# A recurrent attention with a feed-forward behind it: chunk 0 in two units of two batches, second masks on GpSimd or VectorE, and another table of order

## Chip, core, metric

One core of one Trainium2 chip runs the whole program. The metric is the device time of one execution in microseconds (us). Eight executions of the kernel before gave 171.22 to 172.64 us, median 172.0.

## What is computed

Four batches, 8 heads, 768 steps, head size 48. Each head keeps a 48x48 state; at every step it is read with r, decayed by w and increased by the outer product of k and v; the present step enters the output with the weight u. The 3072 x 384 result goes through a feed-forward without a nonlinearity:

```python
for t in range(S):
    kt, vt, rt, wt = (k[:, :, t], v[:, :, t], r[:, :, t], w[:, :, t])
    cur = np.einsum('bhd,bhe->bhde', u[None] * kt, vt)
    y[:, :, t] = np.einsum('bhd,bhde->bhe', rt, state + cur)
    state = wt[:, :, :, None] * state + np.einsum('bhd,bhe->bhde', kt, vt)
...
x = y.transpose(0, 2, 1, 3).reshape(B * S, H * D)      # 3072 x 384
out = ((x @ w1) * (x @ w2)) @ w3 @ w_out               # 384 -> 1024 -> 1024 -> 384
```

## The kernel before

**Tiling.** The 768 steps are cut in six chunks of 128. A *unit* is one chunk of one or two batches, and `UNITS` lists them as (chunk, first batch, batches): chunk 0 has units 0 and 1 of one batch each and unit 2 of two, the other chunks two units of two batches, 13 units in all. A *block* of the feed-forward takes the tokens of one unit (chunk 0) or of two (`BLOCKS`): 128, 128, 256 and five times 512 tokens. w3 and w_out are multiplied once, in the kernel, to w34 (`w34_block`, eight pieces: transpose of a w3 piece L627, product with w_out L639, each copied out by ScalarE or VectorE), so that a block is two products (x w1 and x w2, L938), their product elementwise (ScalarE copies one out, L947; VectorE multiplies it with the other, L951) and one matmul with w34 (L960), copied out (L968) and stored (L973).

**A unit** (`unit`). ScalarE takes the logarithm of w (ln, L669). TensorE forms cumulative sums with the triangle LT, once by rows (cs, L678) and once transposed (ct, L685). ScalarE takes their exponentials (ne, L692; e, L698). VectorE scales k (Kt, L703). TensorE transposes r (trr, L767) and the scaled k (trk, L786); VectorE multiplies r's transpose by e (RT, L772), and ScalarE or VectorE copies k's (KT, L791). TensorE forms the scores of each batch (m, L805). They are masked to the strict lower triangle (msk): VectorE multiplies them from PSUM by a mask (L811), or ScalarE copies them to SBUF (L814) and GpSimd masks them there in place (maff, L817). The tile is Mbf. TensorE multiplies scores by v (y, L849) and, from chunk 1 on, r by the state (ys, L840).

The diagonal term goes another way. r times k (rk, L708) is weighted by u: in the units of chunk 0 (`PE_DIAG`) TensorE transposes rk (L721), multiplies by a block matrix of u (d, L735), and the sums are copied (dcp, L740); elsewhere rk is multiplied by a broadcast u (ruk, L743) and reduced (dg, L747). The result scales v (dv, L749), and VectorE adds the output of y to it (yb, L861). yb is transposed (yt, L878), copied to xT (L883) and feeds the block. State: k times v (kv, L895), added (T, L902), decayed (S, L906), converted (Sc, L908). In the last four units the three transposes are DMAs on SyncE's queue.

u is one row. It is loaded by GpSimd's queue (L543); TensorE spreads it to all partitions (ub, L548 and L550), VectorE and GpSimd build the block matrix from it (ublk, L559 to L565).

**Loads.** `load` brings rows of w, k, r, v of a unit (in chunk 0) or of four batches (later), L579; `wload` brings halves of w1 and w2, quarters of w3, and w_out, L586. All go on GpSimd's queue, but for those in `SP_LOADS`, w of units 0 and 1, on SyncE's. A GpSimd load occupies GpSimd while it is issued. `LOADS` gives them their turn.

**Order.** Nothing is issued where it stands in the text. Each step is put in a list by `op` with its engine, a nominal duration, what it reads and writes, and a number, the sum of three: `prio` from the text, `RANK` of its kind, `STEP` of its name. `schedule` then walks along a nominal time; on each engine, of the steps that are ready and have room in PSUM (`CAPS`), it takes the one of the lowest number. `ENGINE` says on which engine a step runs that has a choice. Each engine executes its list strictly in that order. The tables `RANK`, `STEP` and `ENGINE` are long and are not shown in full; a load's number is

```python
return -10000.0 + (LOADS.index(key) if key in LOADS else 1000 + 10 * int(key.split("_")[1]) + "wkrv".index(key[0]))
```

plus its `STEP`. The triangle LT and the identity I are finished by GpSimd among its loads (L502, L506), the mask by VectorE (L511).

Of the kernel before, what the change touches and what calls it, by code (L numbers as in the profile page):

```python
# [27 lines left out]
    "table": 91258, "ones": 70780, "I128": 2.5, "pads": 147127.5, "rpads": 129663.5, "state0": 193483,  # L28
    "mask": 114325.5, "u": 6, "ub": 85613, "ubc": 115778.5, "ublk": 139994.5, "ublk2": 139582.5, "w1_0": -1,
    "w2_0": -9, "w2_1": 1, "w3_0": -2, "w3_1": -1, "gate": 18300.5, "wt_0": 186936.5, "w3Te_0": 180388.5,  # L30
    "wm_0": 14284.5, "w34e_0": 196262, "wt_1": 188036.5, "w3Te_1": 184064.5, "wm_1": 14355, "w34e_1": 199640,
    "wt_2": 187264.5, "w3Te_2": 180421.5, "wm_2": 16664.5, "w34e_2": 193580, "wt_3": 190065, "w3Te_3": 183294.5,
    "wm_3": 16602.5, "w34e_3": 193341, "wt_4": 190831, "w3Te_4": 186363.5, "wm_4": 21086.5, "w34e_4": 199881.5,
    "wt_5": 190040.5, "w3Te_5": 178239.5, "wm_5": 17262, "w34e_5": 199838.5, "wt_6": 190773, "w3Te_6": 178710.5,
    "wm_6": 22072.5, "w34e_6": 191892.5, "wt_7": 196434, "w3Te_7": 186247.5, "wm_7": 26850, "w34e_7": 198902,
    "rpad3": 110949.5, "win_0": 9, "kin_0": 2, "rin_0": 1, "vin_0": 7, "ln_0": 30931, "cs_0": 150610.5,
    "ct_0": 76350, "ne_0": 143756.5, "e_0": 168276.5, "Kt_0": 277987.5, "rk_0": 5791.5, "rkt_0": 141899.5,
    "rke_0": 160559, "d_0": 138446.5, "dcp_0": 35270, "dv_0": 113183, "trr_0": 168163.5, "RT_0": 130924.5,
    "trk_0": 151420, "KT_0": 176728.5, "m_0_0": 123125, "msk_0_0": 159784, "maff_0_0": 263427.5, "y_0": 179238.5,
    "yb_0": 262883.5, "yt_0": 197545, "xT_0": 274692.5, "kv_0": 92018.5, "T_0": 197296, "S_0": 111557.5,  # L40
    "Sc_0": 119238.5, "a_0_0": 101744, "b_0_0": 93277, "asb_0_0": 161353.5, "abT_0_0": 286641, "a_0_1": 101961,
    "b_0_1": 93964, "asb_0_1": 159579.5, "abT_0_1": 291543.5, "o_0_0": 5590.5, "osb_0_0": 193613.5,
    "store_0_0": 6002.5, "win_1": -4, "kin_1": -5, "rin_1": 3, "vin_1": 5, "ln_1": 30947, "cs_1": 150772,
    "ct_1": 76143, "ne_1": 141159, "e_1": 168318, "Kt_1": 277556.5, "rk_1": 4519, "rkt_1": 141823.5, "rke_1": 161966,
    "d_1": 138542.5, "dcp_1": 37096, "dv_1": 113323.5, "trr_1": 168113, "RT_1": 133329, "trk_1": 151647,
    "KT_1": 179246.5, "m_1_0": 122337.5, "msk_1_0": 159570.5, "maff_1_0": 264349, "y_1": 178903.5, "yb_1": 268439,
    "yt_1": 198092, "xT_1": 270303.5, "kv_1": 92554.5, "T_1": 197456.5, "S_1": 111049, "Sc_1": 120091,
    "a_1_0": 101694.5, "b_1_0": 94039.5, "asb_1_0": 159924.5, "abT_1_0": 286673, "a_1_1": 101907.5, "b_1_1": 94046.5,
    "asb_1_1": 159555.5, "abT_1_1": 287058, "o_1_0": 5697.5, "osb_1_0": 183614.5, "store_1_0": 6383, "win_2": -2,
    "kin_2": -10, "rin_2": -9, "vin_2": 4, "ln_2": 27502, "cs_2": 150899, "ct_2": 77090, "ne_2": 140677,  # L50
    "e_2": 165156, "Kt_2": 277775, "rk_2": 8720.5, "rkt_2": 141179, "rke_2": 159467, "d_2": 138283.5, "dcp_2": 42304,
    "dv_2": 112314.5, "trr_2": 168851, "RT_2": 128671.5, "trk_2": 151531.5, "KT_2": 175478, "m_2_0": 122874.5,
    "msk_2_0": 157605, "maff_2_0": 263855, "m_2_1": 122898.5, "msk_2_1": 162959.5, "maff_2_1": 263536,
    "y_2": 179372.5, "yb_2": 263117, "yt_2": 197797.5, "xT_2": 277998.5, "kv_2": 92588.5, "T_2": 193231,
    "S_2": 110815, "Sc_2": 121324.5, "a_2_0": 102140, "b_2_0": 94251, "asb_2_0": 159794, "abT_2_0": 289379,
    "a_2_1": 103972, "b_2_1": 93111, "asb_2_1": 159681.5, "abT_2_1": 289610, "a_2_2": 101093.5, "b_2_2": 94164.5,
    "asb_2_2": 161243.5, "abT_2_2": 291851.5, "a_2_3": 101827.5, "b_2_3": 93487.5, "asb_2_3": 158664.5,
    "abT_2_3": 291948, "o_2_0": -5503.5, "osb_2_0": 183340.5, "store_2_0": 5875, "o_2_1": 5884.5, "osb_2_1": 182980,
    "store_2_1": 6211.5, "win_3": -3, "vin_3": 3, "ln_3": 27848, "cs_3": 151181, "ct_3": 77556, "ne_3": 140780.5,
    "e_3": 165597.5, "Kt_3": 275543.5, "rk_3": 7878.5, "ruk_3": 74734.5, "dg_3": 9567.5, "dv_3": 75124,  # L60
    "trr_3": 167958, "RT_3": 129021.5, "trk_3": 151855, "KT_3": 178411.5, "m_3_0": 125437, "msk_3_0": 155155,
    "maff_3_0": 225704.5, "m_3_1": 123078.5, "msk_3_1": 160746, "maff_3_1": 264622, "ys_3": 21875, "y_3": 179345,
    "yb_3": 268271.5, "yt_3": 197961.5, "xT_3": 270309, "kv_3": 96277, "T_3": 198817, "S_3": 115528,
    "Sc_3": 123788.5, "ln_4": 27267, "cs_4": 150936.5, "ct_4": 77248, "ne_4": 140824, "e_4": 165405.5,
    "Kt_4": 281230, "rk_4": 7858, "ruk_4": 75130, "dg_4": 6720.5, "dv_4": 116166.5, "trr_4": 168619, "RT_4": 128759,
    "trk_4": 150933.5, "KT_4": 176652.5, "m_4_0": 122915.5, "msk_4_0": 157299, "maff_4_0": 264522.5, "m_4_1": 122692,
    "msk_4_1": 164510, "maff_4_1": 225906, "ys_4": 19313, "y_4": 178859, "yb_4": 268194, "yt_4": 201240.5,
    "xT_4": 274660.5, "kv_4": 96164.5, "T_4": 190408, "S_4": 116763, "Sc_4": 127066, "a_3_0": 110805.5,
    "b_3_0": 107195.5, "asb_3_0": 166326, "abT_3_0": 284054, "a_3_1": 105385.5, "b_3_1": 97538, "asb_3_1": 166241.5,
    "abT_3_1": 284607, "a_3_2": 114695, "b_3_2": 106576.5, "asb_3_2": 166344, "abT_3_2": 297320.5, "a_3_3": 109704,  # L70
    "b_3_3": 107425.5, "asb_3_3": 165812.5, "abT_3_3": 284217.5, "o_3_0": 3065, "osb_3_0": 189965,
    "store_3_0": -13643.5, "o_3_1": -3540.5, "osb_3_1": 182912, "store_3_1": 6189, "o_3_2": 3720.5,
    "osb_3_2": 178613.5, "store_3_2": -13244.5, "o_3_3": 3864.5, "osb_3_3": 190066.5, "store_3_3": -13873,
    "win_5": 92762.5, "kin_5": 92899.5, "rin_5": 93432, "vin_5": 127145.5, "ln_5": 27637.5, "cs_5": 154048.5,
    "ct_5": 83867, "ne_5": 148436.5, "e_5": 172207, "Kt_5": 281438, "rk_5": 3786.5, "ruk_5": 77301, "dg_5": 9607.5,
    "dv_5": 74252, "trr_5": 175681.5, "RT_5": 143863, "trk_5": 159034, "KT_5": 176385.5, "m_5_0": 124511,
    "msk_5_0": 172521, "maff_5_0": 225963, "m_5_1": 131175, "msk_5_1": 162305.5, "maff_5_1": 260791, "ys_5": 20907,
    "y_5": 191985.5, "yb_5": 260626.5, "yt_5": 210295.5, "xT_5": 276599, "kv_5": 94241, "T_5": 191553,
    "S_5": 109235.5, "Sc_5": 126032.5, "ln_6": 34632, "cs_6": 154367, "ct_6": 84620.5, "ne_6": 147704.5,
    "e_6": 170579, "Kt_6": 281133.5, "rk_6": 19597.5, "ruk_6": 77271.5, "dg_6": 1840.5, "dv_6": 74062.5,  # L80
    "trr_6": 181449.5, "RT_6": 126707, "trk_6": 159283.5, "KT_6": 183212.5, "m_6_0": 135160.5, "msk_6_0": 161986,
# [969 lines left out]
```

## Time and profile before

| | |
|---|---|
| median of 8 executions | 172.0 us (171.22 to 172.64) |
| the profiled execution | 172.34 us, span 170.6 us |
| TensorE (PE) busy | 155.2 us, 91%, 1732 matmuls |
| VectorE (DVE) busy | 120.9 us, 71% |
| GpSimd (POOL) busy, issue of loads included | 106.8 us, 63% |
| ScalarE (ACT) busy | 98.0 us, 57% |
| granted TensorE clock | 1.00 throughout |
| moved by DMA | 24.12 MB, 141 GB/s on average |
| chain that ended last | PE 85%, POOL 4%, DMA 4%, DVE 3%, issue 2%, ACT 1% |

How to read it: the span is the time from the first to the last instruction of one profiled execution; the execution's own time is a little longer. Busy time is the sum over an engine's instructions. A line of a group names the source line, the engine, the operation, output and inputs with their shapes, how often it occurred, then busy time and mean duration, and after the second bar the idle time of the engine just before it and what ended it. In the chain each piece is followed back to what released it. "DMA to landing" is from the start of the issuing instruction to the completion of the transfer.

### The profile page before, as it was taken

The page shows a single profiled execution, that of the slowest core. Times are in us where ns is not written, and L with a number is a line of the kernel's source. Part 1 is how long each engine was busy: PE and PEld are TensorE (multiplying, and loading weights), DVE is VectorE, ACT ScalarE, POOL GpSimd, SP SyncE. Part 2 cuts the span into 40 slices and gives each one's busy share as a digit, 9 for nine tenths or more (in the row PEclk, how much of TensorE's full clock was granted, in tenths as well). Part 3 has the DMA queues.
Part 4 walks back from the last instruction along what each step waited for, and adds up shares of the span by engine and source line. Part 5 has one row for each costly group of instructions (what it writes and reads, how often), then busy time and mean ns, then how long its engine had stood idle before and what let it go on. Part 6 is the DMA issues. An engine that isn't in the chain of part 4 may idle for free.

```text
span 170.6 us, 4149 instructions
## 1 busy us (share of the span) xinstructions
PE 155.2 (91%) x1732; PEld 99.9 (59%) x1732; DVE 120.9 (71%) x156; ACT 98.0 (57%) x134; POOL 106.8 (63%) x90
## 2 busy tenths in 40 slices
PE   0543899999999999999999999999999999999991
PEld 0332679998677576656655576456556554455550
DVE  6254899886886689798899987898796770633330
ACT  4522458788754778536869888645574425233311
POOL 7999497975996898999967999915533200000000
PEclk9999999999999999999999999999999999999999
DMA  5999999999999999999999992957365222011132
GB/s 98 134 196 188 225 174 146 167 187 181 180 229 150 144 144 122 131 227 205 169 197 259 152 180 72 136 134 164 82 122 147 96 60 80 4 46 46 46 126 107
DMA packets 96364, 24.12 MB, mean 141 GB/s; under 512 B 88633, under 2 KB 94265, under 8 KB 96345
## 3 DMA queue, kind: packets, MB, share of 16 engines
q0 software_dynamic: 79024, 15.86, 117.7%
q1 hardware_dynamic: 17320, 8.00, 18.7%
q8 instruction: 13, 0.21, 0.5%
q14 instruction: 7, 0.05, 0.1%
HBM read 27.79 MB, written 4.72 MB: 191 GB/s over the span
## 4 chain that ended last, share of the span: by engine, by line
PE 85%; POOL 4%; DMA 4%; DVE 3%; issue 2%; ACT 1%; POOLq 0%; DVEq 0%
PE banks L938 36%; PE banks L960 19%; PE banks L639 6%; PE banks L805 4%; DMA u_row<-in_u_dram 4%; PE banks L849 3%; PE banks L685 3%; PE banks L627 2%; PE banks L895 2%; PE banks L678 2%; PE banks L878 2%; POOL kin L579 2%; PE banks L767 2%; PE banks L786 2%; PE banks L840 1%
## 5 line engine op out<-in xcount | busy, mean ns | idle before, releaser
L938 PE MATMUL banks<-xT,w_bf 128*128 128x512 bf16 (+2 forms) x384 | 68.3, 327 | 0.1
L938 PEld LDWEIGHTS <-w_bf 128*128 128x128 bf16 x384 | 32.8, 98 | 25.4 <-issue 0.6
L951 DVE TENSOR_TENSOR abT<-a_sb,banks 128x1024 bf16<-128x1024 f32 (+1 forms) x28 | 29.7, 1067 | 22.1 <-PE banks L938 18.4
L947 ACT COPY a_sb<-banks 128x1024 f32<-128x1024 f32 (+1 forms) x28 | 24.8, 891 | 16.6 <-PE banks L938 15.6
L960 PE MATMUL banks<-w,abT 128*128 128x384 bf16 x192 | 33.9, 327 | 0.0
L960 PEld LDWEIGHTS <-abT 128*128 128x128 bf16 x192 | 18.3, 98 | 12.8
L968 ACT COPY osb<-banks 128x384 f32<-128x384 f32 x19 | 9.1, 478 | 20.0 <-PE banks L960 18.5
L817 POOL TENSOR_SCALAR_AFFINE_SELECT Mbf<-Mbf 128x1024 bf16<-128x1024 bf16 x12 | 13.0, 1093 | 9.5 <-ACT Mbf L814 9.4
L749 POOL TENSOR_TENSOR dv<-vin,dg 128x768 bf16<-128x768 bf16 (+1 forms) x9 | 12.9, 1443 | 9.0 <-DMA xT<-dv 5.1
L811 DVE TENSOR_TENSOR Mbf<-banks,mask 128x1024 bf16<-128x1024 f32 x12 | 14.6, 1220 | 4.1 <-PE banks L805 2.9
L814 ACT CAST Mbf<-banks 128x1024 bf16<-128x1024 f32 x12 | 12.1, 1017 | 5.4 <-PE banks L805 5.4
L698 ACT ACTIVATE eT<-banks 128x1024 f32<-128x1024 f32 (+1 forms) x13 | 12.5, 959 | 3.1 <-PE banks L685 3.1
L703 DVE TENSOR_TENSOR Kt<-kin,banks 128x768 bf16<-128x768 bf16 (+1 forms) x11 | 9.6, 878 | 5.5 <-DMA kin<-in_k_dram 4.6
L685 PE MATMUL banks<-LT,lw 128*128 128x128 bf16 x96 | 8.3, 234 | 5.5 <-POOL LT L502 5.1
L708 POOL TENSOR_TENSOR rk<-rin,kin 128x768 bf16<-128x768 bf16 x8 | 13.1, 1638 | 0.2 <-DMA rin<-in_r_dram 0.2
L861 DVE TENSOR_TENSOR dv<-banks,dv 128x768 bf16<-128x768 f32 (+1 forms) x13 | 11.6, 893 | 1.7 <-PE banks L849 1.3
L692 ACT ACTIVATE banks<-banks 128x768 f32<-128x768 f32 (+1 forms) x13 | 9.7, 750 | 4.5 <-PE banks L678 4.5
L579 POOL DMA_DIRECT2D vin<-in_v_dram x7 | 10.0, 1423 | 2.6 <-issue 2.6
L772 DVE TENSOR_TENSOR KRT<-banks,eT 128x1024 bf16<-128x1024 bf16 (+1 forms) x9 | 9.9, 1103 | 2.1 <-PE banks L767 1.1
L639 PE MATMUL banks<-wo_bf,w3T 128*128 128x384 bf16 x64 | 11.4, 327 | 0.0
L579 POOL DMA_DIRECT2D kin<-in_k_dram x7 | 10.0, 1436 | 1.1 <-POOLq L1035 0.8
L685 PEld LDWEIGHTS <-lw 128*128 128x128 bf16 x96 | 6.8, 105 | 6.4 <-ACT lw L669 4.3
(92 smaller groups left out, 234.3 us busy)
## 6 DMA issues: line engine op xcount, KB each, us to landing
out_dram<-osb SPq DMA_DIRECT2D x24, 192.0 KB, 2.0
win<-in_w_dram POOLq DMA_DIRECT2D x4, 768.0 KB, 8.8
w_bf<-in_moe_w_dram POOLq DMA_DIRECT2D x4, 512.0 KB, 7.5
w_bf<-in_moe_w_dram POOLq DMA_DIRECT2D x4, 384.0 KB, 7.7
kin<-in_k_dram POOLq DMA_DIRECT2D x4, 384.0 KB, 7.9
rin<-in_r_dram POOLq DMA_DIRECT2D x4, 384.0 KB, 8.1
vin<-in_v_dram POOLq DMA_DIRECT2D x4, 384.0 KB, 8.4
wo_bf<-in_moe_w_out_dram POOLq DMA_DIRECT2D x1, 768.0 KB, 8.6
```

Source lines behind the costliest of these rows:

```text
L579: op(eng, 60 if eng == "SP" else 650 + 270 * nb, lambda: e.dma_start(dst[:, b0 * H:(b0 + nb) * H, :D], ap), late=SP_ROWS if src == "w" and ...
L639: nc.tensor.matmul(o[:, :DM], lhsT=w3T[fi % 2][:, gi, :], rhs=wo_bf[:, gi, :], start=(gi == 0), stop=(gi == FI - 1))
L685: nc.tensor.matmul(o[:, b, q, :], lhsT=LW[:, b * H + 2 * q:b * H + 2 * q + 2, :].rearrange("t h d -> t (h d)"), rhs=LT, start=True, stop=True)
L698: nc.scalar.activation(ET[:, :, 1:], o[:, :nb * HP, :], Act.Exp)
L708: op("DVE", {"DVE": dve(N, 2), "POOL": 1490}, lambda e: ENG[e].tensor_mul(rks, rr[:, :, :D], kk), r=[*kr, *kk_], w=[f"rk{s}"], prio=pr + 8 ...
L749: op("POOL", {"POOL": 100 + 1.8 * N, "DVE": dve(N)}, lambda e: ENG[e].tensor_mul(dvs, vv, dgs[:, :, None].to_broadcast([C, bh, D])), r=[f" ...
L811: nc.vector.tensor_mul(Mbf[m].rearrange("s j q t -> s (j q t)"), o.rearrange("s j f -> s (j f)"), mask.rearrange("s q t -> s (q t)"))
L817: nc.gpsimd.affine_select(Mbf[m].rearrange("s j q t -> s (j q) t"), Mbf[m].rearrange("s j q t -> s (j q) t"), compare_op=Alu.is_gt, fill=0 ...
L938: nc.tensor.matmul(o[:, q * T // TB, q % (TB // T), :], lhsT=wt[:, di, fi * P:(fi + 1) * P], rhs=xT[x][:, di, :T], start=(di == 0), stop=( ...
L947: nc.scalar.copy(a_sb[sa][:, :nbk * TB], banks[:, g.at(A):g.at(A) + nbk, :].rearrange("p k t -> p (k t)"))
L951: nc.vector.tensor_mul(abT[x][:, f[0]:f[0] + G, :T].rearrange("p i t -> p (i t)"), a_sb[sa][:, :nbk * TB], banks[:, g.at(Bk):g.at(Bk) + nb ...
L960: nc.tensor.matmul(banks[:, g.at(O), :DM], lhsT=abT[x][:, fi, tt * P:(tt + 1) * P], rhs=w34[:, fi, :], start=(fi == 0), stop=(fi == FI - 1))
```

## The change

- Chunk 0 has two units of two batches. There are 12 units (numbered 0 to 11), and the blocks of chunk 0 have 256 tokens each. Unit 1 now holds what unit 2 held. The sets that name units are shifted with it.
- SyncE loads w of unit 0 (two batches in one DMA); all else is on GpSimd's queue.
- The halves of w1 and w2 come before the rows of chunk 1 in `LOADS`. (The sizes of the weight pieces stay: `WP` is 2, `W3P` is 4.)
- The second step of a mask that ScalarE copied out can run on VectorE, as a product with the mask in SBUF.
- `RANK`, `STEP` and `ENGINE` are replaced, so the order of all engines changes. By the new `ENGINE`, 9 masks are made by VectorE from PSUM and 15 copied by ScalarE; of those, 10 are masked by GpSimd and 5 by VectorE.

```diff
 STEP = {
...
+    "w3Te_0": 179236, "wm_0": 28425, "w34e_0": 182625, "wt_1": 203756.5, "w3Te_1": 171253, "wm_1": 28573.5,
...
 ENGINE = {
...
+    "rke_0": "DVE", "dcp_0": "ACT", "dv_0": "DVE", "KT_0": "ACT", "msk_0_0": "DVE", "maff_0_0": "POOL",
+    "msk_0_1": "ACT", "maff_0_1": "DVE", "xT_0": "DVE", "S_0": "DVE", "osb_0_0": "DVE", "osb_0_1": "ACT",
...
-LOADS = """win_0 kin_0 u rin_0 vin_0 win_1 kin_1 rin_1 vin_1 win_2 kin_2 rin_2 vin_2
-w1_0 w2_0 w1_1 w2_1 win_3 kin_3 rin_3 vin_3 wo w3_0 w3_1 w3_2 w3_3""".split()
-
-UNITS = [(0, 0, 1), (0, 1, 1), (0, 2, 2)] + [(c, b, 2) for c in range(1, 6) for b in (0, 2)]
-
-DMA_KR = set(range(9, 13))
-DMA_Y = set(range(9, 13))
-DMA_R = set(range(9, 13))
-PE_DIAG = {0, 1, 2}
+LOADS = """win_0 kin_0 u rin_0 vin_0 win_1 kin_1 rin_1 vin_1 w1_0 w2_0 w1_1 w2_1
+win_2 kin_2 rin_2 vin_2 wo w3_0 w3_1 w3_2 w3_3""".split()
+
+UNITS = [(0, 0, 2), (0, 2, 2)] + [(c, b, 2) for c in range(1, 6) for b in (0, 2)]
+
+DMA_KR = set(range(8, 12))
+DMA_Y = set(range(8, 12))
+DMA_R = set(range(8, 12))
+PE_DIAG = {0, 1}
...
-BLOCKS = [[0], [1], [2], [3, 4], [5, 6], [7, 8], [9, 10], [11, 12]]
-
-SP_LOADS = {("w", 0), ("w", 1)}
+WP, W3P = 2, 4
+
+BLOCKS = [[0], [1]] + [[t, t + 1] for t in range(2, 12, 2)]
+
+SP_LOADS = {("w", 0)}
...
-            def maff(m=m):
+            def maff(e, m=m):
+                if e == "DVE":
+                    nc.vector.tensor_mul(Mbf[m].rearrange("s j q t -> s (j q) t"), Mbf[m].rearrange("s j q t -> s (j q) t"), mask)
+                    return
                 nc.gpsimd.affine_select(Mbf[m].rearrange("s j q t -> s (j q) t"), Mbf[m].rearrange("s j q t -> s (j q) t"),
                                         compare_op=Alu.is_gt, fill=0.0, base=0, channel_multiplier=-1,
                                         pattern=[[0, 2 * HP], [1, C]])
...
-            op("POOL", 1110 * by_act, maff if by_act else lambda: None, r=[f"M{m}"], w=[f"M{m}"], prio=pr + 7 + b,
+            op("POOL", {"POOL": 1110 * by_act, "DVE": 690 * by_act}, maff if by_act else lambda e: None, r=[f"M{m}", "mask"], w=[f"M{m}"], prio=pr + 7 + b,
                name=f"maff_{t}_{b}", port=True)
```

The loads up to chunk 1, in the order of their numbers (those in brackets are on SyncE's queue; LT and I stand among them by their own numbers):

| | |
|---|---|
| before | kin_2, kin_1, (win_1), rin_2, LT, kin_0, rin_0, w2_0, I, win_2, u, (win_0), rin_1, vin_0, w1_0, vin_1, win_3, w1_1, vin_2, w2_1, kin_3, rin_3, w3_0, wo, w3_1, vin_3, w3_2, w3_3 |
| after | kin_0, rin_0, vin_0, LT, win_1, I, kin_1, (win_0), u, rin_1, vin_1, w1_0, w2_0, w2_1, w1_1, win_2, w3_0, kin_2, rin_2, wo, w3_1, w3_2, w3_3, vin_2 |

In a name such as kin_2 the number is the unit's; from chunk 1 on the load of a chunk's first unit brings all four batches (win_3 before is win_2 after).

## The prediction

> **What bounds the kernel now.** I read the slices of the page first, then busy time by stretch, then TensorE's own waits, then the chain that ended last. In the slices (one digit is the busy share of 4.27 us, in tenths) TensorE is the row to watch:
>
> ```profile
> PE   0543899999999999999999999999999999999991
> DVE  6254899886886689798899987898796770633330
> POOL 7999497975996898999967999915533200000000
> ```
>
> From the sixth slice to the last but one TensorE is full; before that it is not. The stretches give the size (columns: stretch, its length, then PE, PEld, DVE, ACT, POOL busy, granted clock, DMA share, GB/s):
>
> ```profile
> 5.00:10.00 5.00, 2.29 (x15) 1.43 (x15) 1.83 (x4) 2.45 (x5) 5.00 (x8) 1.00 2.43 139
> 10.00:15.00 5.00, 1.94 (x19) 1.60 (x20) 2.50 (x4) 0.58 (x1) 5.00 (x6) 1.00 1.52 203
> 15.00:20.00 5.00, 4.19 (x48) 2.92 (x48) 3.47 (x9) 2.18 (x5) 2.75 (x6) 1.00 1.34 223
> 20.00:25.00 5.00, 4.62 (x55) 3.89 (x52) 4.97 (x6) 2.53 (x4) 5.00 (x4) 1.00 1.62 188
> 30.00:40.00 10.00, 10.00 (x153) 9.22 (x151) 8.17 (x11) 8.17 (x11) 7.06 (x6) 1.00 1.35 182
> 160.00:170.60 10.60, 7.20 (x44) 4.01 (x41) 2.89 (x4) 1.41 (x3) 0.00 (x0) 1.00 0.26 95
> ```
>
> TensorE is idle 15.44 us of 170.6 (170.6 - 155.16): 5.00 before the first matmul, 2.71 + 3.06 + 0.81 + 0.38 up to 25 us, 0.1 up to 160, and 3.4 at the end, where the last copy and store follow the last matmul. Nothing is to be had in the middle; the start is the only stretch with idle TensorE, and DMA and GpSimd's issues fill it. TensorE's waits name the causes:
>
> ```profile
> PE banks L685 <- POOL LT L502: 5.1, 1, 5.1
> PE banks L548 <- DMA u_row<-in_u_dram: 2.7, 1, 2.7
> PE banks L786 <- DVE Kt L703: 2.6, 2, 1.4
> ```
>
> The chain shows how the start ends (start, length, what):
>
> ```profile
> 8.92 6.19 DMA u_row<-in_u_dram
> ...
> 18.29 1.23 DVE Mbf L811
> ...
> 20.74 2.06 DVE dv L749
> ...
> 25.18 1.58 PE banks L938 x24
> ...
> 27.82 0.67 PE banks L938 x12
> ...
> 36.92 0.65 PE banks L938 x6
> ```
>
> The row u lands at 15.1; from there the diagonal term, dv, yb, yt and xT lead to the first feed-forward matmul at 25.18.
>
> **TensorE's total: nothing.** Units (0,0,1) and (0,1,1) become one, with the same matmuls per batch. Only the feed-forward of chunk 0 changes form: 96 matmuls of 128 columns and 48 of 256 become 96 of 256. The chain has 12 of 128 in 0.67 (56 ns) and 6 of 256 in 0.65 (108 ns), so 96 x 0.056 = 5.4 us become 48 x 0.108 = 5.2: 0.2 gained. The Trainium skill (TensorE: Matmul & The Clock Gate, Back-to-back issue gap) gives about 81 ns for a 128-column matmul with its weight load; by it the narrow form would cost 7.8 us and the change would gain 2.6. The row is from this very line, so I take 0.2.
>
> **Masks.** The rows that price them:
>
> ```profile
> L811 DVE TENSOR_TENSOR Mbf<-banks,mask 128x1024 bf16<-128x1024 f32 x12 | 14.6, 1220 | 4.1 <-PE banks L805 2.9 <-issue 1.1
> L814 ACT CAST Mbf<-banks 128x1024 bf16<-128x1024 f32 x12 | 12.1, 1017 | 5.4 <-PE banks L805 5.4
> L817 POOL TENSOR_SCALAR_AFFINE_SELECT Mbf<-Mbf 128x1024 bf16<-128x1024 bf16 x12 | 13.0, 1093 | 9.5 <-ACT Mbf L814 9.4
> L511 DVE TENSOR_TENSOR mask<-LT,I 128x1024 bf16<-128x1024 bf16 x1 | 0.7, 693 | 0.0
> ```
>
> By the engine table, direct masks on VectorE go from 12 to 9, ScalarE copies from 12 to 15; behind these, GpSimd masks 10 and VectorE 5. The new form has no row; L511, same shape and types, gives 0.69. (Bounds: not below this; 1.22 if it ran at L811's pace, 2.7 us for five, on an engine with 50 us idle.) VectorE: -3 x 1.22 + 5 x 0.69 = -0.2; GpSimd -2 x 1.09 = -2.2; ScalarE +3 x 1.02. With all other reassignments in the table, priced from the same rows, VectorE has +1.6 us, ScalarE -3.1, GpSimd -1.7. What matters is the crowded stretch, 60 to 100 us, where VectorE is busy 36.3 of 40 us and GpSimd 36.8. For the four units of chunks 2 and 3: VectorE +2.8 (four second masks) +0.5 (rk) -1.3 (ruk) -1.9 (S) -0.6 (xT) = -0.5; GpSimd -4.4 (masks) -1.6 +3.3 +1.9 = -0.8. So TensorE's cover holds and this costs nothing. A VectorE mask waits for ScalarE's copy, and the abT and yb behind it wait too; a miss costs at most the 1.02 of one copy each, five in all.
>
> **The load queue.** A load's place is -10000 plus its index in LOADS plus STEP. Before, GpSimd issues the rows of unit 2 first (kin_2, kin_1, rin_2), then LT, kin_0, rin_0, w2_0, I, win_2, u. After: kin_0, rin_0, vin_0, LT, win_1, I, kin_1, u, rin_1, vin_1, then w1_0, w2_0, w2_1, w1_1, win_2, w3_0, kin_2, rin_2, wo, w3_1 to w3_3, vin_2. (Unit 1 after holds the batches of unit 2 before.) SyncE's two loads of w become one of two batches, which I put at 4.4, where the second of the two lands now. On GpSimd k, r and v of batches 0 and 1 are one issue of 1.2 us each instead of two of 0.9: 1.8 less. Asked one at a time, the loads of before land: kin_2 6.5, rin_2 8.5, kin_0 9.3, rin_0 10.0, u 15.1, w1_0 17.7, win_3 21.8, w2_1 26.7, kin_3 29.8, rin_3 32.1, wo 39.1, vin_3 45.4, w3_3 50.8; successive landings stand 1.3 us apart for two batches of rows and some 2 us for a w1 or w2 half. In the new order this gives estimates of kin_0 6.5, rin_0 7.8, vin_0 9.1, LT 5.35 (5.06 now), win_1 10.9, kin_1 12.3, u 14.0 (ends 12.6 and 14.4: GpSimd issues it at 8.2, and u now takes 6.2), vin_1 15.1, w1_0 17.2, w2_0 19.2, w1_1 23.3 to 24.8, win_2 26.4, kin_2 32, rin_2 34.5, wo 38.7, w3_3 47, vin_2 50. So chunk 0's rows come earlier, w3 too, and chunk 1's rows later: w and v by 4.6 us, k and r by 2.3.
>
> **The start, after.** ln needs both batches: 4.45 to 5.3, so cs begins at 5.4 (5.11 now) but for two batches; Kt ends near 9.2 for both (9.9 now), RT and KT near 10.4, scores at 11.4. u then decides. From u's landing to the first feed-forward matmul it takes 10.0 us now, of which the steps themselves are 4.9 and 5.1 is queueing: Mbf 1.23 and Kt 0.95 ahead on VectorE, and dv at 2.06 where the row of 768 elements elsewhere shows 0.96. After, steps for two batches are 5.5 (u 0.74, ublk 0.7, d 0.35, dg 0.2, dv 0.96, yb 0.96, yt 0.5, xT 0.55, nine handovers of 0.06). Of the queueing I keep half, 2.5, as two units compete and not three. First feed-forward matmul: 14.0 + 5.5 + 2.5 = 22.0.
>
> What counts is time minus work done. Warm pieces of the chain give 8.4 us for all of chunk 0's attention and u. Chain and idle from 25.18 to 167.21 leave 5.7 done by 25.18: 19.5 lost. After, at 22.0, of unit 1 the scores, y, kv, d and yt are open (1.9): 6.5 done, 15.5 lost. Gain 4.0.
>
> **What is given back.** TensorE at the start runs at half pace:
>
> ```profile
> 20.85 1.03 PE L767 MATMUL banks<-I,rin 128*128 128x128 bf16 x8
> ...
> 35.86 0.61 PE L767 MATMUL banks<-I,rin 128*128 128x128 bf16 x8
> ```
>
> The same eight transposes take 1.03 and then 0.61; now it is warm from 25.5. The Trainium skill (same page, What's actually happening) speaks against this change: full pace comes after about 3.4 us of sustained work, and an idle window of that length takes it away. By it the 3.4 us after 22.0 run at half pace: 1.7 lost. By the rows alone (dense from 19.6, warm at 25.5) it can be up to 2.9, or nothing if unit 1's attention has warmed it. I take 0.8. Between 30 and 50 us TensorE lives on rows of chunk 1 and the w3 work as they land; I take 0.4 for gaps (0 to 2.5). Sum: 4.0 + 0.2 - 0.8 - 0.4 = 3.0. The profiled execution was 172.34 (span 170.6 and 1.74 around it), so 169.3 for such a one; the median of eight is 172.0, so **169.0**.
>
> **Rivals.** *Loads late* (0.20): w1_1 and win_2 come behind four weight halves; feed-forward 0 stops after its first half, TensorE waits to 24.8, cools, and again for kin_2 and wo. For it: every load issued from 12.86 to 17.02 us took 8.9 to 9.7 to land. Against: before has a similar queue and no wait on it after 16 us. Price 1.5 + 0.8 more: 171.3. *u decides as now* (0.08): u lands at 15 and the queueing stays 5.1; feed-forward at 25.6 with 6.5 to 7 done, 172 within 0.5: no change. *Slower* (0.17): vin_2 is last on GpSimd's queue, behind masks and dv. From v's landing to chunk 1's first feed-forward now passes 9.3 us (45.4 to 54.74). TensorE's other work (8.4 + 10.4 feed-forward 0 + 14.0 w3 work + 7.4 attention 1 + 5.2 outputs 0 = 45.4, with 15.5 lost) lasts until 60.9, so vin_2 later than 51.6 costs its lateness, and later than about 54.6 all the gain; GpSimd has waited 5.5 us at once for a mask's copy. At 57: 174.4. Against: a backlog of some 6 us of transfers covers such a wait. *Main case* (0.55): 167.4 to 170.6.
>
> **Chances and range.** A measurement tells 0.3% from no change, some 0.5 us. Faster: 0.53 of the main case, 0.18 of late loads, 0.02 of the third, together 0.73; same 0.02 + 0.01 + 0.04 = 0.07; slower 0.17 + 0.01 + 0.02 = 0.20. From 166.8 (no loss to cold or gaps, u at 12.6) to 173.4, which leaves most of the slow case and a little below out.
>
> **What would show it.** Right: the first L938 near 22; u landing near 14; TensorE's idle sum near 12.5; no L938 wait for w_bf; L811 x9, L814 x15, L817 x10 and five bf16 masks near 0.7. Wrong: TensorE idle between 25 and 60 us, waits of vin or abT, five masks well over 1 us, or a first L938 after 24.

## The result, and the profile after

The changed kernel takes **171.28 us** (median of 18 runs, 170.55 to 171.82); the kernel before 171.99 us (53 runs, 171.22 to 173.15). The ratio is 0.995, 95% interval 0.9934 to 0.9966: faster by 0.7 us, where the prediction had 3.0 us. The ratio of a variant, below, is taken against runs of the kernel before made together with it; ratios leave out executions over 1.5% slower than the fastest of their kernel, which medians count. Its profiled execution took 171.36 us with a span of 169.6; that of before 172.34 with 170.6.

Lines have moved in kernel.py: the feed-forward products L938 are now L942, the w34 product L960 is L964, the cumulative sums L685 and L678 are L686 and L679, the transposes L767 and L786 are L768 and L787, the scores L805 are L806, the masks L811, L814, L817 are L812, L815, L821, and L819 is VectorE's second mask. The other lines move by 1 ahead of the masks and by 4 behind them: y is L853, yb L865, yt L882, kv L899.

The slices of the page, each now 4.24 us:

```profile
PE   0488899998999999999799999999998999999991
DVE  5378786788367999997898999985896573415510
POOL 7995589069989987997999999526332400000000
```

TensorE is fuller in slices 3 to 5 than it was (4 3 8 before, 8 8 8 now), but there are now slices below 9 behind the sixth: the tenth, the twentieth, the thirty-first. Those were all 9 before. Busy time by stretch (stretch, length, then PE, PEld, DVE, ACT, POOL busy, granted clock, DMA share, GB/s):

```profile
10.00:15.00 5.00, 3.74 (x56) 2.70 (x54) 3.79 (x7) 3.47 (x5) 3.12 (x5) 1.00 2.36 150
20.00:25.00 5.00, 4.28 (x49) 3.33 (x48) 4.45 (x6) 2.95 (x5) 4.43 (x4) 1.00 1.14 240
25.00:30.00 5.00, 4.81 (x61) 3.92 (x60) 2.74 (x5) 3.92 (x6) 4.38 (x5) 1.00 1.83 180
30.00:40.00 10.00, 9.32 (x140) 7.99 (x140) 8.44 (x11) 8.41 (x12) 4.72 (x4) 1.00 1.73 189
80.00:100.00 20.00, 18.89 (x202) 11.09 (x199) 17.25 (x21) 16.08 (x21) 19.39 (x14) 1.00 2.02 180
160.00:169.60 9.60, 6.05 (x38) 3.43 (x35) 1.99 (x3) 1.44 (x3) 0.00 (x0) 1.00 0.28 103
```

TensorE is idle 14.5 us (169.6 less 155.1), 0.9 less than before; 12.5 was forecast. Up to 25 us idle time fell from 12.0 to 8.4. But from 25 to 160 us it grew from 0.1 to 2.5: 0.19 in 25 to 30, 0.68 in 30 to 40, 1.11 in 80 to 100, 0.53 in 120 to 140.

TensorE's own waits:

```profile
PE banks L679 <- POOL LT L503: 5.4, 1, 5.4
PE banks L549 <- DMA u_row<-in_u_dram: 1.3, 1, 1.3
PE banks L882 <- DVE dv L865: 1.1, 1, 1.1
PE banks L768 <- DMA rin<-in_r_dram: 1.1, 1, 1.1
PE banks L942 <- DVE xT L887: 0.7, 1, 0.7
```

The wait for u has gone from 2.7 to 1.3, and Kt's 2.6 is off the list. New are L882 (yt), 1.1 us for yb (L865, written into the tile dv), which itself waits for GpSimd's dv (L750), and 0.5 us of the scores L806 for a ScalarE mask copy (L815):

```profile
PE banks L806 <- ACT Mbf L815: 0.5, 1, 0.5
```

The chain that ended last now runs through the middle of the kernel on other engines than TensorE:

```profile
7.85 5.54 DMA u_row<-in_u_dram
...
22.08 10.05 DMA kin<-in_k_dram
...
74.49 1.49 POOL dv L750
...
77.21 1.72 POOL kin L580
...
79.81 1.44 POOL dv L750
```

**Where the gain was, and where it went.** Idle time does not see a TensorE that runs at half pace. So I also took the elapsed time less the work done: each matmul of the trace counts with its own form's start-to-start time at full pace (56 ns for 128 columns, 109 for 256, 162 for 384, 216 for 512), and the rest is lost. (A few records are missing in traces, which makes it uncertain by some 0.2 us.)

| us lost by | 25 us | 40 | 60 | 80 | 90 | 120 | 160 |
|---|---|---|---|---|---|---|---|
| before | 19.0 | 19.75 | 20.6 | 21.3 | 21.1 | 22.7 | 23.5 |
| after | 14.8 | 16.8 | 17.5 | 18.35 | 19.6 | 21.35 | 22.6 |
| gain | 4.2 | 2.95 | 3.1 | 2.95 | 1.5 | 1.35 | 0.9 |

The start brings 4.2 us. 1.3 goes back between 25 and 40 us, nothing from 40 to 80, 1.4 between 80 and 90, 0.6 later (0.53 of it idle at 128 us, behind one multiplication on VectorE that took 2.44 us instead of 1.21 beside a GpSimd operation; in the traces of five variants it took 1.22, so this part is one execution's).

### The profile page after: what moved, and what is told of

It reads as the page before. It is cut to its first block, busy times and chain, and to the rows that moved or that the text cites. A ratio compares the mean times of both kernels' runs of the same rounds, so it can differ in the third digit from the quotient of the medians.

```text
span 169.6 us, 4034 instructions
## 1 busy us (share of the span) xinstructions
PE 155.1 (91%) x1684; PEld 99.0 (58%) x1684; DVE 120.9 (71%) x156; ACT 96.2 (57%) x124; POOL 102.6 (60%) x85
## 4 chain that ended last, share of the span: by engine, by line
PE 68%; POOL 12%; DMA 11%; issue 4%; DVE 2%; ACT 1%; POOLq 0%; DVEq 0%
PE banks L942 26%; PE banks L964 16%; PE banks L640 6%; DMA kin<-in_k_dram 6%; DMA u_row<-in_u_dram 3%; POOL dv L750 3%; PE banks L853 2%; POOL kin L580 2%; PE banks L686 2%; PE banks L806 2%; PE banks L787 2%; PE banks L679 2%; PE banks L768 2%; DMA KRT<-Kt 2%; PE banks L628 2%
## 5 line engine op out<-in xcount | busy, mean ns | idle before, releaser
L942 PE MATMUL banks<-xT,w_bf 128*128 128x512 bf16 (+1 forms) x336 | 67.8, 349 | 1.2 <-DVE xT L887 0.7
L942 PEld LDWEIGHTS <-w_bf 128*128 128x128 bf16 x336 | 31.7, 98 | 27.1 <-issue 1.6
L951 ACT COPY a_sb<-banks 128x1024 f32<-128x1024 f32 (+1 forms) x28 | 24.9, 890 | 26.2 <-PE banks L942 23.5
L964 PE MATMUL banks<-w,abT 128*128 128x384 bf16 x192 | 34.5, 326 | 0.0
L964 PEld LDWEIGHTS <-abT 128*128 128x128 bf16 x192 | 18.1, 98 | 12.6
L821 POOL TENSOR_SCALAR_AFFINE_SELECT Mbf<-Mbf 128x1024 bf16<-128x1024 bf16 x10 | 11.0, 1097 | 12.6 <-ACT Mbf L815 11.7
L750 POOL TENSOR_TENSOR dv<-vin,dg 128x768 bf16<-128x768 bf16 x9 | 13.2, 1476 | 7.6 <-DMA xT<-dv 5.5
L815 ACT CAST Mbf<-banks 128x1024 bf16<-128x1024 f32 x15 | 14.9, 1016 | 2.7 <-PE banks L806 2.6
L865 DVE TENSOR_TENSOR dv<-banks,dv 128x768 bf16<-128x768 f32 x12 | 11.5, 955 | 6.0 <-PE banks L853 3.8
L812 DVE TENSOR_TENSOR Mbf<-banks,mask 128x1024 bf16<-128x1024 f32 x9 | 11.0, 1220 | 2.8 <-PE banks L806 2.6
L693 ACT ACTIVATE banks<-banks 128x768 f32<-128x768 f32 x12 | 9.5, 798 | 5.8 <-PE banks L679 5.7
L699 ACT ACTIVATE eT<-banks 128x1024 f32<-128x1024 f32 x12 | 12.3, 1026 | 0.5 <-PE banks L686 0.4
L679 PE MATMUL banks<-lw,LT 128*128 128x384 bf16 x24 | 6.5, 357 | 5.4 <-POOL LT L503 5.4
L744 POOL TENSOR_TENSOR rk<-rk,u_bc 128x768 bf16<-128x768 bf16 x6 | 10.2, 1704 | 0.3
L773 DVE TENSOR_TENSOR KRT<-banks,eT 128x1024 bf16<-128x1024 bf16 x8 | 9.6, 1220 | 0.7 <-issue 0.4
L670 ACT ACTIVATE lw<-win 128x768 bf16<-128x768 f32 x10 | 8.2, 839 | 3.1 <-DMA win<-in_w_dram 3.1
L792 ACT COPY KRT<-banks 128x1024 bf16<-128x1024 bf16 x7 | 7.1, 1015 | 4.9 <-PE banks L787 4.9
## 6 DMA issues: line engine op xcount, KB each, us to landing
w_bf<-in_moe_w_dram POOLq DMA_DIRECT2D x4, 512.0 KB, 10.8
```

The lines of the kernel that those rows point to most:

```text
L699: nc.scalar.activation(ET[:, :, 1:], o[:, :nb * HP, :], Act.Exp)
L750: op("POOL", {"POOL": 100 + 1.8 * N, "DVE": dve(N)}, lambda e: ENG[e].tensor_mul(dvs, vv, dgs[:, :, None].to_broadcast([C, bh, D])), r=[f" ...
L812: nc.vector.tensor_mul(Mbf[m].rearrange("s j q t -> s (j q t)"), o.rearrange("s j f -> s (j f)"), mask.rearrange("s q t -> s (q t)"))
L815: nc.scalar.copy(Mbf[m].rearrange("s j q t -> s j (q t)"), banks[:, g.at(MM):g.at(MM) + 2, :])
L821: nc.gpsimd.affine_select(Mbf[m].rearrange("s j q t -> s (j q) t"), Mbf[m].rearrange("s j q t -> s (j q) t"), compare_op=Alu.is_gt, fill=0 ...
L865: nc.vector.tensor_add(ybs.rearrange("t b (q e d) -> t e (b q) d", e=2, d=D), o, dvs.rearrange("t (b q e) d -> t e (b q) d", b=nb, e=2))
```

## Experiments

Each variant keeps the planner's order of instructions but for the moves named. In the diffs `move(a, b, 0)` puts step a ahead of step b in the program, `move(a, b, 1)` behind it, and `step(a)` is the step of that name. "Earlier at 40 us" compares the same TensorE instruction in two traces.

### Does the start's gain come from the units or from the order of loads?

**The kernel before, with rows of batches 0 and 1 first.**

```
+    move("I128", "LT", 1)
+    move("rin_1", "rin_0", 1)
+    move("u", "rin_1", 1)
+    move("vin_0", "w2_0", 1)
+    move("win_2", "vin_0", 1)
+    move("kin_2", "win_2", 1)
+    move("rin_2", "kin_2", 1)
```

> The kernel before with its own units, and with the loads of batches 0 and 1 (k, r, then u) ahead of w, k and r of batches 2 and 3: the order of loads alone, without merging the units. Theory (fewer and larger pieces of work give the earlier start, as rows and u are worth nothing one at a time): the first feed-forward matmul at 24 to 25.5 us (25.1 before) and the time within 0.4 us of 172.0. Rival (the start was bound by loads in the wrong order): first feed-forward matmul at 21 to 22.5 us, and the time 171.0 to 171.5, all that the change brought.

Measured: 171.66 us, ratio 0.9967 (0.9942 to 0.9992). In the timeline of TensorE (start, length, line, operands, count, wait):

```profile
19.70 0.41 PE L895 MATMUL banks<-vin,Kt 128*64 128x48 bf16 x8 [1.49 <-DMA vin<-in_v_dram]
...
24.30 2.44 PE L938 MATMUL banks<-xT,w_bf 128*128 128x128 bf16 x24
```

TensorE is 4.8 us earlier at 15 us, but 0.8 at 23 us and 0.02 from 27 us on: v of batch 1, pushed back by the move, is the next to be late, and the first feed-forward matmuls run at half pace (24 in 2.44 us, 1.65 before). This order did not bring the start that the changed kernel has. It is one order of many, and by the ratios alone (0.9967 against 0.995, with overlapping intervals) the two could not be told apart; the trace can. Whether the larger units or the order that the new tables give them make the start early is not settled by it.

**The kernel before, with u's load early.**

```
+    move("u", "LT", 1)
```

> The kernel before with the load of u issued right behind LT, ahead of kin_0, instead of behind win_2; nothing else moves. Theory (loads bind only a TensorE that is some 2 us ahead of the kernel before; the kernel before waits for no load after 16 us): the wait of 2.7 us for u at 12.4 goes, the first feed-forward matmul comes 1 to 2.5 us earlier, and 0.7 to 2 us of it stay: 170.0 to 171.3. Rival (any gain at the start is waited for by 40 us in either kernel): within 0.4 of 172.0.

Measured: 172.27 us, ratio 1.0007 (0.998 to 1.0033). TensorE's waits:

```profile
PE banks L767 <- DMA rin<-in_r_dram: 3.0, 1, 3.0
PE banks L786 <- POOL I L506: 1.6, 1, 1.6
```

The wait for u is gone; r of batch 1 takes its place. At 15 us TensorE is 2.7 us earlier, at 18 us 0.1. In the kernel before, u was the last of several loads that were all late.

**The changed kernel, with the rows of batches 2 and 3 first.**

```
+    move("kin_1", "kin_0", 0)
+    move("rin_1", "kin_0", 0)
```

> The changed kernel with the loads of k and r of batches 2 and 3 (kin_1, rin_1) issued ahead of kin_0, as the kernel before issues them first; nothing else moves. Theory (the start is gained by the order of the row loads): kin_0 and rin_0 land about 2.6 us later, at 8.8 and 10.6, the first feed-forward matmul moves from 20.9 to 22.5 to 23.5, and the time rises by 1 to 2.5 us, to 172.3 to 173.8. Rival (the start is gained by two larger units in place of three, so fewer pieces stand in the queues): the first feed-forward matmul stays within 0.7 us of 20.9 and the time within 0.5 of 171.3.

Measured: 170.97 us, 0.995 (0.9924 to 0.9976). TensorE begins 2.3 us late (LT is 2.3 later on GpSimd's queue), the first feed-forward matmul is at 21.80 instead of 20.86, and the delay melts: 0.97 at 20 us, 0.62 at 40, nothing behind 82. A start that is 1 us worse costs nothing at the end.

**The changed kernel, with u's load first among the small ones.**

```
+    move("u", "rin_0", 0)
```

> The changed kernel with the load of the row u issued right after kin_0 instead of behind kin_1; nothing else moves. Theory (a gain at the start that frees TensorE is kept to the end apart from waits that it does not touch): the wait of 1.26 us for u at 13.4 goes, rin_0 and all later loads come 0.5 us later, the first feed-forward matmul comes 0.5 to 1.2 us earlier, and the time falls by 0.3 to 1.0. Rival (from 25 to 40 us the landing of w1, of chunk 1's rows and of w_out sets the pace, so what TensorE gains before is waited for there): first feed-forward matmul earlier, time the same or up to 0.5 us longer.

Measured: 170.51 us, 0.9918 (0.9888 to 0.9948). The first feed-forward matmul is at 19.12, TensorE 1.75 us earlier at 23 us, and then:

```profile
23.27 1.49 PE L942 MATMUL banks<-xT,w_bf 128*128 128x256 bf16 x12 [0.71 <-DMA w_bf<-in_moe_w_dram]
...
27.34 0.62 PE L686 MATMUL banks<-LT,lw 128*128 128x128 bf16 x8 [0.53 <-ACT lw L670]
...
30.43 0.62 PE L628 MATMUL banks<-I,w_bf 128*128 128x128 bf16 x8 [0.83 <-DMA w_bf<-in_moe_w_dram]
```

It waits for w1's second half, for chunk 1's w, whose load ends just before lw can be made, and for w3's first quarter; by 32 us it is 0.2 us *later* than the changed kernel. So a start that is 1.75 us better is worth nothing at 32 us, as one that is 1 us worse was soon made good. This has the lowest median of the kernels that compute the whole, but its interval overlaps that of the changed kernel, and its trace is only 0.2 us ahead from 82 to 125 us (behind that, it is also spared the 0.6 us at 128); that it is better is not shown.

### What takes the gain back between 25 and 40 us?

**u first, and less to load.** The second half of w1 is left out, and the products of the second half use the first half's columns again: the output is another, the instructions are the same.

```
+    move("u", "rin_0", 0)
+    order.remove(step("w1_1"))
...
-            op("PE", cost, lambda K=A, f=fis: fill(K, w1_bf, f), ...
+            op("PE", cost, lambda K=A, f=fis: fill(K, w1_bf, [x % 4 for x in f]), ...
```

> The kernel with u's load first, and with the second half of w1 not loaded at all: the first half's columns are used twice, so the feed-forward part computes something else with the same instructions. 0.79 MB less go through the queue before w, k, r of chunk 1. Theory (between 20 and 40 us TensorE runs into load landings, w and k of chunk 1 above all): chunk 1's w lands by 25 us instead of about 27, its k by 30 instead of 32, the waits at 26.6 and 29.3 us are gone, and at 40 us TensorE's instructions are 1.0 to 2.0 us earlier than in the kernel with u first; at the end 0.5 to 1.5 us of it are left (169.0 to 170.0). Rival (the losses after 25 us come from the evacuating engines and not from loads): no instruction at 40 us moves by more than 0.4 us, and the time is 170.3 to 170.8.

Measured: **169.44 us**, 0.9826 (0.9794 to 0.9859), against 170.51 and 0.9918 (0.9888 to 0.9948) with u first alone; the intervals do not overlap. The piece of the chain for chunk 1's k (issue, us to landing), with u first alone and then with less to load:

```profile
20.64 11.72 DMA kin<-in_k_dram
```

```profile
20.86 9.81 DMA kin<-in_k_dram
```

k lands at 30.7 instead of 32.4, and TensorE is 1.75 us earlier at 32 us, 1.55 at 40 and 55, and 0.9 from 82 us to the end. The three waits above are gone or shorter (0.2 for the w of chunk 1's sums). This is the theory's case with nearly all its numbers (k was to land by 30), and it shows what the better start ran into: from 22 to 35 us TensorE follows the landings of w1, w, w3 and k.

The changed kernel itself loses something else besides. Of the 2.0 us that it loses between 25 and 40, the waits for lw and for Kt behind the landings of chunk 1's w and k are 0.6, by the paces above. More is lost where the four score products of chunk 1 (L806) stand close together on TensorE and three of them are copied out by ScalarE in a row:

```profile
37.98 2.84 ACT L815 CAST Mbf<-banks 128x1024 bf16<-128x1024 f32 x3 [0.40 <-PE banks L806]
```

```profile
39.96 0.40 PE L806 MATMUL banks<-KRT 64*128 64x128 bf16 x8 [0.52 <-ACT Mbf L815]
```

From 37.98 to 40.29 TensorE does 1.0 us of work in 2.3. The kernel before also copies three of these four, but spreads its scores from 38.6 to 43.8 among feed-forward products, and has no such wait. The wait of 0.52 stands in the trace with less to load too, as in those of all ten variants of the changed kernel. No run moves these scores or copies, so that this loss would go with another order is read from the trace and not tested.

### What takes it back at 80 us?

**The load of chunk 4's k behind dv of unit 4, on GpSimd's queue.**

```
+    move("kin_8", "dv_4", 1)
```

> The changed kernel with one step moved on GpSimd: the load of k for chunk 4 (kin_8) goes behind dv of unit 4 instead of ahead of it; every other order stays. Theory (part of the gain of the start is lost at 80.9 us because dv of unit 4 stands on GpSimd behind a load that waits and is issued for 1.23 + 1.72 us): dv starts near 76.0 instead of 79.75, the wait of TensorE for yb at 82.28 (1.1 us) goes, and the time falls by 1.0 to 1.2 us, to about 170.2. Rival (TensorE's stalls replace one another, since vector work or loads set the pace of this stretch): a wait of about the same size comes within the next 20 us, and the time stays within 0.3 us of 171.3.

GpSimd's timeline in the changed kernel:

```profile
74.49 1.49 POOL L750 TENSOR_TENSOR dv<-vin,dg 128x768 bf16<-128x768 bf16 x1
77.21 1.72 POOL L580 DMA_DIRECT2D kin<-in_k_dram  x1 [1.23 <-DVE abT L955]
78.95 0.86 POOL L910 TENSOR_TENSOR Sst<-Tst,eT 128x384 f32<-128x384 f32 x1
79.75 1.48 POOL L750 TENSOR_TENSOR dv<-vin,dg 128x768 bf16<-128x768 bf16 x1
```

and with the move:

```profile
74.23 1.53 POOL L750 TENSOR_TENSOR dv<-vin,dg 128x768 bf16<-128x768 bf16 x1
75.74 0.83 POOL L910 TENSOR_TENSOR Sst<-Tst,eT 128x384 f32<-128x384 f32 x1
76.54 1.47 POOL L750 TENSOR_TENSOR dv<-vin,dg 128x768 bf16<-128x768 bf16 x1
77.96 1.72 POOL L580 DMA_DIRECT2D kin<-in_k_dram  x1
...
95.50 1.10 POOL L821 TENSOR_SCALAR_AFFINE_SELECT Mbf<-Mbf 128x1024 bf16<-128x1024 bf16 x1
```

dv of unit 4 starts at 76.54 instead of 79.75, and TensorE's wait at 81 us (L882, 1.1) is gone: relative to the changed kernel it goes from 0.6 late to 0.7 early across this place, 1.3 gained. That shows what held dv back: a load issue of 1.72 us and 1.23 us of idle ahead of it on the same queue. (What the issue itself waited for in those 1.23 us is open: the operation that the profile names ended at 76.6.) But between 96 and 100 us 0.7 is given back. GpSimd comes to the mask shown last at 95.50, as it does in the changed kernel (95.54); TensorE is earlier and now waits for it (0.20), and then for Kt (0.15). Measured: 170.77 us, 0.993 (0.9904 to 0.9957): 0.2% under the changed kernel, which the intervals cannot tell from none.

**Both moves at once.**

```
+    move("u", "rin_0", 0)
+    move("kin_8", "dv_4", 1)
```

> Both single moves at once: u's load first among the small ones, and the load of k of chunk 4 behind dv of unit 4. Theory (each move takes away one wait, and what it wins is taken back by the next one in line): about 170.2 us, below either move alone (170.8 and 170.5) by no more than 0.4, with TensorE's wait for dv at 81 us gone and a wait for a GpSimd mask near 97 us. Rival (the two gains are independent and add up): 169.5 to 169.8. Second rival (the movements of 0.3 us are noise): 170.9 to 171.3.

Measured: 171.04 us, 0.9937 (0.9913 to 0.996): neither my sum nor the rival's, but the third case, no better than the changed kernel. The trace has the new wait at full size:

```profile
PE banks L853 <- POOL Mbf L821: 1.0, 1, 1.0
```

From 1.4 us early at 90 us TensorE comes to 0.4 late at 100; 1.2 of these 1.8 are lost at this mask, which GpSimd starts at 96.21. Two moves that each take away a stall that is plain in the trace do not add up.

### Can another queue take the loads?

**w of chunks 3, 4 and 5 on SyncE's queue instead of GpSimd's.**

```
+    for t in (6, 8, 10):
+        step(f"win_{t}").fn = lambda t=t: nc.sync.dma_start(win[...], w of that chunk)
```

> The changed kernel with the loads of w for chunks 3, 4 and 5 (no conversion) moved from GpSimd's queue to SyncE's, at the same places of the order. Theory (GpSimd is what is late from 60 to 82 us: issuing loads, and waiting in them for earlier loads to land): 2 x 1.73 us of issue and the wait of 1.23 go from its queue ahead of dv of unit 4, dv starts near 75 instead of 79.75, the wait at 82.28 goes, and since kin_8 is not put off, nothing comes back at 97 as it did when kin_8 was moved behind dv; 0.8 to 1.4 us less than the changed kernel, 169.9 to 170.5. Rival (the 16 DMA engines are what is full, not the queue that feeds them): rows of k, r and v come later by as much as w takes, and the time stays within 0.4 of 171.3.

Measured: 178.16 us, 1.0333 (1.03 to 1.0366): the theory missed by 8 us. GpSimd is freed of three issues, but TensorE stands still at 72 us:

```profile
PE banks L899 <- DMA vin<-in_v_dram: 7.1, 1, 7.1
```

This v of chunk 3 stays on GpSimd's queue, issued at 61.44, and takes 18.3 us to land; in the changed kernel no load of rows takes more than 10.8. The DMA engines are full in this stretch (9 tenths in the page's slices up to 100 us), and with the second queue they moved 162, 138 and 135 GB/s from 65 to 70, 75 and 80 us, against 166, 188 and 213 in the changed kernel: the second queue added no bandwidth, and this v got less of it. SyncE also issues the two loads of w earlier than GpSimd did (64.0 and 64.5 instead of 66.1 and 72.7), so two loads of w are under way with this v at once; the run does not separate the second queue from that. TensorE then ran at a granted clock of 0.50 from 77.1 to 83.9 us, and was 9.1 us late at 80. The Trainium skill (DMA: Bandwidth & Descriptors, SWDGE vs HWDGE vs iDMA) says that each DMA engine takes turns between its queues; the 18.3 us agree with that.

**u first, and chunk 1's w on SyncE's queue**, issued only once yb of unit 0 is done (a one-element write on VectorE holds it back):

```
+    move("u", "rin_0", 0)
+    step("win_2").fn = ... nc.sync.dma_start(...)
+    move("win_2", "yb_0", 1)
```

> The changed kernel with the row u loaded right after kin_0, and w of chunk 1 (win_2) loaded by SyncE's queue once yb of unit 0 is done, instead of by GpSimd behind w1_1 (a one-element write of VectorE into that tile holds it back until then). Theory (after the start, the landing of w1, w3 and chunk 1's rows from GpSimd's queue is what TensorE waits for at 22, 27, 30 and 32 us): the queue has 384 KB less ahead of w3_0 and kin_2, so of the 1.75 us that u first gained at 23 us and lost by 32, 1.0 or more is still there at 40; 169.5 to 170.3. Rival (the DMA engines are full whatever the queue): all of it is lost by 40 again, 170.5 to 171.3.

Measured: 178.0 us, 1.0315 (1.0276 to 1.0354). Here the moved load itself is the late one: `lw` of chunk 1 keeps TensorE waiting 6.2 us from 27.8. The load was issued at 18.5 us, 2.7 later than with u first alone; how much of the loss is that, and how much the shared engines, is open.

**Both together.** 

> Both of the above together: u right after kin_0, and w of chunks 1, 3, 4 and 5 on SyncE's queue. Theory (two separate places where loads on GpSimd hold TensorE): the gains add, 1.5 to 2.6 us less than the changed kernel, 168.7 to 169.8. Rival (what is gained early is waited for later): no better than the better of the two alone.

Measured: 187.16 us, 1.0765 (1.0717 to 1.0812; this ratio is about 185 us): both losses together, whose sum would be 1.07.

### Do the new masks matter?

**The five masks of ScalarE and VectorE put back to one instruction on VectorE.**

```
+    for t in ("0_1", "4_0", "5_0", "6_1", "7_0"):
+        step(f"msk_{t}").eng = "DVE"
+        order.remove(step(f"maff_{t}"))
```

> The five masks that the changed kernel does in two steps, ScalarE's copy and VectorE's multiplication (one 1.02 us and 0.68 to 2.15 us), are put back to one VectorE instruction that reads PSUM, at the place of the copy; nothing else moves. ScalarE loses 5 x 1.02 = 5.1 us of work, VectorE gains 5 x 1.22 less the five multiplications that it had (about 6.1 us of work for 6.0). Theory (the masks' place decides nothing, as the prediction had it: TensorE's work covers them): 171.0 to 171.6 us, within 0.3 of the changed kernel, and no TensorE instruction after 60 us off by more than 0.5 us. Rival (the two-step masks took load off the engine that TensorE waits for, and are a part of the gain): 172.0 us or more, with new waits for Mbf or for VectorE between 65 and 105 us. Second rival (the two-step masks are a loss, through the multiplications that ran beside GpSimd at 1.7 and 2.15 us): 170.3 to 170.8.

Measured: 171.7 us, 0.9989 (0.9961 to 1.0017), beside 0.995 (0.9934 to 0.9966): between theory and first rival, with overlapping intervals. In the trace TensorE has a new wait at 71 us (`PE banks L942 <- DVE Mbf L812`, 0.9), as two masks of 1.2 us stand one behind the other on VectorE; 1.0 of delay comes there and goes again at 81, where the changed kernel waits for dv anyway. So the masks' form gives 0.4 us by the medians and 0.4% (0.7 us) by the ratios, and that it gives anything is not settled. A loss is not to be seen.

**The same five second masks on GpSimd.**

```
+    for o in order:
+        if o.kind == "maff" and o.dur:
+            o.eng = "POOL"
```

> The changed kernel with the five second masks of VectorE put on GpSimd at the same places of the order. Theory (GpSimd's queue is what is late between 65 and 82 us): two of the five stand ahead of dv of units 4 and 5, 1.09 us each, so the wait at 82.28 grows from 1.1 to about 3 us, and the first adds about 0.4 to 1 at the start; 172.5 to 174. Rival (as predicted: the masks lie beside other work, and VectorE's mask of 2.15 us at 67.9 is no gain over GpSimd): 171.3 within 0.5.

Measured: 171.78 us, 0.999 (0.9961 to 1.0018). I had expected GpSimd's queue to hold dv back further; it did not (L882 starts at 82.37, in the changed kernel at 82.28), and a loss of 0.8 came elsewhere, at 97 us, where y waits 0.64 for a mask on GpSimd. This trace is also 0.8 us late at 40 us, but its granted clock was 0.50 from 14.2 to 24.5 us, so that is no price of the masks; it is gone at 82.

## Why the prediction was right and wrong

**TensorE's total (0.2 gained): right.** In the new trace twelve matmuls of 256 columns start over 1.31 us, 109 ns each, against the 108 taken. The row of 56 ns for 128 columns, and not the skill's 81, was the price to use: the further 2.4 us of gain that 81 would give are not there.

**Masks (nothing): right within what was measured.** From the page, and for L819 from the view of the tile Mbf (min, median, max in ns):

```profile
L821 POOL TENSOR_SCALAR_AFFINE_SELECT Mbf<-Mbf 128x1024 bf16<-128x1024 bf16 x10 | 11.0, 1097 | 12.6 <-ACT Mbf L815 11.7
...
L815 ACT CAST Mbf<-banks 128x1024 bf16<-128x1024 f32 x15 | 14.9, 1016 | 2.7 <-PE banks L806 2.6
...
L812 DVE TENSOR_TENSOR Mbf<-banks,mask 128x1024 bf16<-128x1024 f32 x9 | 11.0, 1220 | 2.8 <-PE banks L806 2.6
```

```profile
L819 DVE TENSOR_TENSOR Mbf<-Mbf,mask x5: 677/827/2145, 13.4 to 102.2; 128x1024 bf16<-128x1024 bf16 x5
```

Counts and prices came as written, but two of the five took 1.71 and 2.15 us, above the bound of 1.22 that I had set. No matmul waited for them. The wait of 0.5 at 40 us is for a copy of ScalarE, of which chunk 1 has three in both kernels; it belongs to the order, which this step did not price.

**Loads and start (gain 4.0): right, better by about 1.** LT came at 5.33 (5.35 forecast), u at 13.4 (14.0), chunk 1's w at 27.1 (26.4), its k at 32.1 (32), its r at 35.0 (34.5), its v at 49.4 (50). The first feed-forward matmul is at 20.86 (22.0), and 4.2 us are gained by 25 us where 4.0 less 0.8 for the cold start were forecast. The 0.8 was not paid: TensorE reached full pace at 19.9, before that matmul and not after it. That was luck: in the trace of the variant with its masks on GpSimd, whose first feed-forward matmul comes at 19.97, it was not before 24.5. The two runs on the kernel before agree with the step's reason: neither u nor the rows alone gave this start there; what did (units or order) they do not show.

**What is given back (0.4 for gaps): this is the step that failed.** It measured 3.3, and the text put it in two places. First, "between 30 and 50 us TensorE lives on rows of chunk 1 and the w3 work as they land; I take 0.4". I had the landings of chunk 1's rows right to 0.7 us and still charged only a few gaps; 1.3 us went between 25 and 40. One mistake was to carry the gain of the start forward as a sum, when TensorE's next work has a date of its own: an earlier TensorE only meets the same landing sooner. The run with less to load shows it, 1.75 us at 32 us; the runs with a better and a worse start show it from the other side. The other was to leave out the order of chunk 1's scores and copies, where the larger part of the loss before 40 us lies; that part is read from the trace only. TensorE idle between 25 and 60 us was a sign of being wrong that I had named; it was 0.9 us, 0.5 of it for a copy. The rival of late loads named a part of the mechanism, but placed it at w1 and before 25 us; that its 171.3 is the measured time is chance. Second, "so TensorE's cover holds and this costs nothing", for 60 to 100 us. It was argued from sums by engine (GpSimd 0.8 us less busy). GpSimd was busy 36.8 of 40 us there, and on an engine so full it is the place in the queue that counts: a load issue ahead of dv cost 1.3 us. No sum over a stretch can show that. Taking this one wait away shows what it cost, and also that most of it is not won at the end (170.77 us): the next mask has its date too. The remaining 0.6 is the multiplication at 128 us, in one execution.

**The slower rival (v of chunk 1 behind GpSimd's work)** did not come: v landed at 49.4, before the 51.6 us from which it would have cost, and TensorE was idle 0.04 us between 40 and 60.

So the sum 4.0 + 0.2 - 0.8 - 0.4 became, in the profiles, 4.2 by 25 us (no cold start to take off) less 3.3: 0.9, and 0.7 in the medians.

## What to carry to other kernels

A gain at the start of a kernel is worth what is left of it at the next resource with a date of its own: before adding it to the end, list the load landings and full queues behind it, and cut the gain at each. Where an engine is busy nine tenths of a stretch, read its queue in order for what the critical engine waits for; the engine's sum does not show it. And when two kernels differ by a few tenths of a per cent, compare the times of identical instructions along the two traces: they show gains of over 1 us being won and lost that the medians hide.

## What the runs showed of the hardware

**The pace of TensorE at the start is not fixed by the program.** Three variants (u first; the same with less to load; both moves) issue the same TensorE instructions in the first 20 us with landings within 0.7 us, but by their start-to-start times they came to full pace for good at 11.5, 16.8 and 18.8 us; the changed kernel did at 19.9. The second and the third had full pace already from 9.9 and 12.0 us and lost it for 3.4 us. For the third (by stretch, as above; the granted clock is the 0.50):

```profile
12.00:15.40 3.40, 2.01 (x40) 1.60 (x35) 3.40 (x8) 3.10 (x5) 1.74 (x5) 1.00 2.18 163
15.40:18.80 3.40, 3.31 (x49) 3.06 (x49) 3.12 (x4) 2.13 (x4) 2.48 (x3) 0.50 1.20 188
```

Eight matmuls of 128 columns took 0.61 us before this spell and 1.01 in it. In the changed kernel and in the one before the granted clock reads 1.00 through the whole start, though eight of them took 1.03 until 19.9 and 25.4 us; there only the start-to-start times tell of half pace.

The Trainium skill (TensorE: Matmul & The Clock Gate, What's actually happening) has the clock follow free-running windows of 3.4 us: a busy one gives full pace, an idle one takes it away. The length of the spell fits. So does the changed kernel, which ran 6.5 us without a wait before it had full pace (13.4 to 19.9): two windows, 6.8 us, is the longest that a first whole one can take (an estimate from the page's figure). But the stretch ahead of the spell was not idle: TensorE was busy 2.01 of its 3.40 us, and the variant with u first alone kept full pace through one with 2.10 of 3.41 (11.54 to 14.95 us). Where the limit lies is open; one spell more or less is worth up to 1.7 us at this place (half of 3.4), and a forecast of a start should hold that.

**A VectorE multiplication beside GpSimd.** The same mask took 0.68 us and 2.15 us. The long one started at 67.88, just behind a GpSimd multiplication that ran from 67.82 for 1.65 us: the rest of that, 1.59, and then 0.68 would be 2.27. The one of 1.71 started at 102.17, beside one that ran from 101.69 to 103.33: 1.16 and 0.68 would be 1.84. The skill (SBUF — State Buffer, SBUF: two separate sides) says that the two engines share a port pair that one of them holds for a whole instruction while the other waits; both numbers agree, to 0.13 us. I had left it out of the mask's bounds.
